# Spectral mixing weights in 4 KB rows: two half-partition loads per tile and block-diagonal stationaries

## The chip, the cores and the metric

One core of one Trainium2 chip runs the whole program. The metric is device time in microseconds of one launch; times are medians over runs. The kernel before takes 456.05 us (three runs: 455.77, 456.05, 456.72).

## What is computed

Linear attention with an exponential feature map, followed by a spectral mixing layer over the sequence. Cut to what matters:

```python
# q, k, v: (8 batches, 8 heads, 576, 64) f32; w_phi (64, 128)
phi(x) = concat(exp(p), exp(-p))          # p = x @ w_phi - max|x @ w_phi|
kv  = k_p^T v ; z = sum(k_p)              # per batch and head
x   = (q_p kv) / (q_p z)                  # (8, 576, 512): heads side by side
X   = rfft(x, axis=1)[:, :64]             # 64 modes
Yr  = Xr w_r - Xi w_i                     # per mode: (8 x 512) @ (512 x 512)
Yi  = Xr w_i + Xi w_r                     # w_r, w_i: (64, 512, 512) f32
u   = x + irfft(Y)
out = u + relu(u @ w_ch)                  # w_ch (512, 512)
```

The mode weights w_r and w_i are 64 x 512 x 512 floats each, 134 MB together; q, k and v are 9.4 MB each. Every weight is used once.

## The kernel before

The 512 input rows of each mode's matrix are the 8 heads times 64. The kernel treats them in four quarters g of 128 rows (two heads). The first quarter is split in its two heads, the others are whole.

**Attention loop** (lines 555 to 623). There are N = 32 units of work: 8 units of two batches and one head (quarter 0), then 24 units of one batch and two heads (quarters 1 to 3). Iteration n works on unit n (`feat_tok`, `feat_q`, `exps`, `ekq`), on unit n-1 (`kv_mm`, `num_mm`, `numer`) and on unit n-2 (`x_mm`). The order on each engine is the order in which this code is written (`manual_schedule`); the framework adds the waits. `vscale` (L270, L275), on POOL, scales v of unit n and writes `vaug`, which `kv_mm` of unit n (L286, TensorE) reads in iteration n+1. `numer` ends with the unit's part of x in `xs_all`. `x_mm` (L344) multiplies that by the cosine and sine columns `CF4` and ScalarE copies the result into `XT` (L369): the modes of x, with 32 columns per mode and part (real, imaginary; 8 batches), beside columns of zeros, so that a stationary of 32 columns fills either the upper or the lower half of a 32-row output block. There are two such buffers, `XT0` and `XT1`, used by quarters in turn. In iterations 28 to 33 `flip_early` and `times_w_early` do pieces of x @ w_ch; `inverse_matrix` runs in iterations 10 to 14.

**Weights** come in 32 groups (`weights`, L156): 8 groups of 16 modes for the two heads of quarter 0 (L167: four loads of 64 partitions), then 24 groups of 8 modes, `wr` and `wi` (L162: one load of 128 partitions each). The loads convert f32 to bf16 and are issued on POOL's queue. `wr` and `wi` have three buffers each (`NW = 3`): the load of group k+3 waits until `mode_mm` of group k (L390, TensorE, 16 matmuls at L416 per group) has read its buffer. `mode_sum` (VectorE) adds the result to `Yacc`. In the loop one group is multiplied per iteration once its quarter of x is there (`after`, L111: groups 0 to 3 from iteration 5, 4 to 7 from 9, 8 to 15 from 17, 16 to 21 from 25).

**POOL's order in one iteration** (from n = 4): the loads of q and k for a later pair of units (`load_qk`, L143, odd n), then the weight loads for which a buffer may become free (L585 to 587), then `vscale`. v is loaded from SP's queue (L127), and is not converted.

**The tail** (lines 785 to 819) multiplies the last ten groups, 22 to 31, and between them does the other x @ w_ch pieces (`flip_x`, `times_w`) and, for quarter 3, the turn of Y by batch (`by_batch`). After group 31 come the inverse transform and the output (lines 841 to 856).

Of the kernel before, what the change touches and what calls it, by code (L numbers as in the profile page):

```python
# [21 lines left out]
NCH = 5  # L22
# [4 lines left out]
def kernel(  # L27
# [11 lines left out]
    nc = tc.nc  # L39
# [14 lines left out]
    xs_all = pers.tile([128, B_ * NCH, DMODEL], BF16, name="xs_all")  # L54
# [8 lines left out]
    CF4 = const.tile([128, NCH, 4, 64], BF16, name="CF4")  # L63
# [3 lines left out]
    XTs = [XT0, XT1]  # L67
# [23 lines left out]
    def qk_pair(pool, i):  # L91
        return [pool.tile([128, 2, 10, D_], BF16, name=f"{nm}2_{i}") for nm in "qk"]
# [63 lines left out]
    def weights(k):  # L156
        g, gi = groups[k]
        wt = {}
        for ri, w in ((0, moe_w_r), (1, moe_w_i)):
            t = pw.tile([128, 8, DMODEL], BF16, name=f"w{'ri'[ri]}", tag=f"w{ri}")  # L160
            if gi >= 0:
                nc.gpsimd.dma_start(  # L162
                    t, w[8 * gi:8 * gi + 8, g * 128:(g + 1) * 128, :].rearrange("m p e -> p m e"))
            else:
                for x in range(2):
                    mx = 16 * (-1 - gi) + 8 * x
                    nc.gpsimd.dma_start(  # L167
                        t[64 * x:64 * x + 64],
                        w[mx:mx + 8, g * 64:(g + 1) * 64, :].rearrange("m p e -> p m e"))
            wt[ri] = t  # L170
        W[k] = wt
# [172 lines left out]
    def x_mm(st):  # L344
        psx = psum.tile([128, 2, 4, 64], F32, name="psx", tag="tx", bufs=1)
        XT = XTs[st["xt"]][:, 16:80, :].rearrange("p (x y b) m -> p x y b m", x=2, y=4)
        if "bs" in st:

            h = st["h"]
            for i, b in enumerate(st["bs"]):  # L350
                for c in range(NCH):
                    for x in range(2):
                        nc.tensor.matmul(
                            psx[64 * x:64 * x + 64, i, :, :],
                            lhsT=xs_all[:, b * NCH + c, h * 64:(h + 1) * 64],
                            rhs=CF4[:, c, :, :],
                            start=(c == 0), stop=(c == NCH - 1),
                        )
        else:
            g = st["g"]  # L360
            for c in range(NCH):
                nc.tensor.matmul(
                    psx[:, 0, :, :],
                    lhsT=xs_all[:, st["b"] * NCH + c, g * 128:(g + 1) * 128],
                    rhs=CF4[:, c, :, :],
                    start=(c == 0), stop=(c == NCH - 1),
                )
        for i, b in enumerate(st["bs"] if "bs" in st else (st["b"],)):
            nc.scalar.copy(  # L369
                XT[:, :, 0:2, b, :],  # L370
                psx[:, i, :, :].rearrange("d (x y) m -> d x y m", x=2),
            )
# [17 lines left out]
    def mode_mm(k, tag="yr"):  # L390
        g, gi = groups[k]
        XT = XTs[1 - g if k < 8 else g % 2]
        wt = W.pop(k)
        if gi < 0:
            psY = psum.tile([128, 2, DMODEL], F32, name="psY2", tag="pC", bufs=1)
            for par in range(2):
                for ri in range(2):
                    for j in range(4):
                        for x in range(2):
                            r = slice(64 * x, 64 * x + 64)  # L400
                            m = 16 * (-1 - gi) + 8 * x + 2 * j + par
                            c0 = (16, 0, 48, 32)[2 * ri + par]
                            nc.tensor.matmul(
                                psY[32 * j:32 * j + 32, x, :],
                                lhsT=XT[r, c0:c0 + 32, m],
                                rhs=wt[ri][r, 2 * j + par, :],
                                start=(par == 0 and ri == 0), stop=(par == 1 and ri == 1),
                            )
            return psY
        psY = psum.tile([128, DMODEL], F32, name="psY", tag=tag, bufs=1)  # L410
        for ri in range(2):
            for par in range(2):
                for j in range(4):
                    m = 8 * gi + 2 * j + par
                    c0 = (16, 0, 48, 32)[2 * ri + par]
                    nc.tensor.matmul(  # L416
                        psY[32 * j:32 * j + 32, :],
                        lhsT=XT[:, c0:c0 + 32, m],
                        rhs=wt[ri][:, 2 * j + par, :],
                        start=(par == 0 and ri == 0), stop=(par == 1 and ri == 1),  # L420
                    )
        return psY

# [26 lines left out]
    def zeros(i):  # L450
        for z in (0, 32, 64):
            nc.vector.memset(XTs[i][:, z:z + 16, :], 0.0)

    def setup():

# [73 lines left out]
    with tc.manual_schedule():  # L529
        load(S[0], "qk")  # L530
        setup()
        load(S[0], "v")
        load(S[1])
        zeros(1)
        casts(S[0], nc.vector)
        casts(S[1], nc.gpsimd, "q")
        load_qk(1)
        for t in AAs:
            nc.gpsimd.memset(t[:, 0, :, 1152:1216], 1.0)
        for t in e2s:  # L540
            nc.gpsimd.memset(t[64:128, :, NCH - 1:NCH], 1.0)
        casts(S[1], nc.gpsimd, "k")

        pa_first_cm.__exit__(None, None, None)
        pa_last_cm = tc.tile_pool(name="pa_last", bufs=1)
        pa_last = pa_last_cm.__enter__()
        qk2s[2] = qk_pair(pa_last, 2)
        for t in qk2s[2]:
            nc.gpsimd.memset(t[:, :, 9, :], 0.0)
        load_qk(2)  # L550
        weights(0)
        k_in = 1
        transp(S[0], "q")
        transp(S[0], "k")
        for n in range(N + 2):
            cur = S[n] if n < N else None
            prev = S[n - 1] if 0 <= n - 1 < N else None
            old = S[n - 2] if 0 <= n - 2 < N else None
            nxt = S[n + 1] if n + 1 < N else None
            if n + 2 < N:  # L560
                load(S[n + 2])
            if cur:
                feat_tok(cur, "k", "pB")
                feat_q(cur)
            if psY is not None:
                mode_sum(k_out, psY)
                psY = None
                k_out += 1
            if cur:
                rem_mm(cur)  # L570
                absmax(cur, "k")
                absmax(cur, "rem")
                exps(cur, "q")
            if nxt:
                transp(nxt, "q")
            if prev:
                kv_mm(prev)
                kv_cp(prev)
            if cur:
                ekq(cur, "k")  # L580
            if n < 4:
                vscale(cur)
            if n % 2 == 1 and 5 <= n < N - 5:
                load_qk((n + 5) // 2)
            while k_in < min(k_out + NW, 2 if n < 3 else 32):  # L585
                weights(k_in)
                k_in += 1
            if n in (1, 3):
                load_qk((n + 5) // 2)
            if n == 16:  # L590
                nc.gpsimd.dma_start(wchb, moe_w_ch.rearrange("(dc p) e -> p dc e", p=128))
            if cur and n >= 4:
                vscale(cur)
            if nxt:
                transp(nxt, "k")
            if cur:
                exps(cur, "k")
                exps(cur, "rem")
            if prev:
                num_mm(prev, 1)  # L600
                numer(prev, 0)
                num_mm(prev, 0)
                numer(prev, 1)
                numer(prev, 2)
            if old:
                x_mm(old)
            e = n - (N + 2 - N_EARLY)
            if e >= 0:
                sTe = flip_early(e)
            if cur:  # L610
                feat_tok(cur, "q", "pA")
                absmax(cur, "q")
                ekq(cur, "q")
            if n == 0:
                forward_matrix()
            if n == 2:
                zeros(0)
            if 10 <= n < 10 + NCH:
                inverse_matrix(n - 10)
            if e >= 0:  # L620
                times_w_early(e, sTe)
            if k_out < K_IN_ATTN and n >= after[k_out] + 2:
                psY = mode_mm(k_out)
# [161 lines left out]
    with tc.manual_schedule():  # L785
        plan = {22: 3, 23: 3, 24: 2, 25: 2, 26: 2, 27: 1, 28: 2, 29: 1, 30: 1, 31: 0}
        while k_out < 32:
            k = k_out
            gi = groups[k][1]
            while k_in < min(k_out + NW, 32):  # L790
                weights(k_in)
                k_in += 1
# [94 lines left out]
```

## Time and profile before

| | before |
|---|---|
| median of 3 runs | 456.05 us |
| span of the profiled execution | 456.7 us (its run is nearest to 456.72) |
| busy PE / VectorE / ScalarE / POOL | 301.7 / 292.0 / 261.8 / 198.8 us |
| mean rate of the DMA engines (as written) | 214 GB/s |
| read from HBM, written | 163.64 MB, 9.44 MB |
| POOL's loads (q0) | 75,728 packets, 76.75 MB |
| loop ends, `mode_mm(22)` starts | 331.07 us |
| last group, `mode_mm(31)` | 415.56 us |

The profile is of one execution. Its times count from the first instruction. "Busy" is the time in which an engine has an instruction at work; a share of busy time is an average over the loop, the tail and the output, which have different limits. The rate of the DMA engines counts bytes as written, so a converting load reads twice what is shown. For a load, "landing" is the moment at which its completion is signalled. In timelines the columns are start, duration, engine, line, operation, and in brackets the idle time before it and what ended that.

### The profile page before, as it was taken

To read this page: it belongs to the slowest core of one execution; us is meant where nothing else is said; L and a number is where in the kernel's file an instruction comes from. 1 tells how busy PE (TensorE), PEld (TensorE's weight loads), DVE (VectorE), ACT (ScalarE), POOL (GpSimd) and SP (SyncE) were. 2 spreads that over 40 slices of the span, in tenths; PEclk is the share of its full clock that TensorE was granted. 3 is DMA by queue.
4 is the path that set the end of the run, shared out by engine and by line. 5 is a ranking of instruction groups with operands and counts; after the bars stand their busy time and mean duration, and the time that the engine had idled before them with its cause. 6 is when DMAs were issued, how large, how long until landed. Compare 5 with 4: busy or idle time off the path is not lost.

```text
span 456.7 us, 11065 instructions
## 1 busy us (share of the span) xinstructions
PE 301.7 (66%) x4637; PEld 197.6 (43%) x4637; DVE 292.0 (64%) x418; ACT 261.8 (57%) x528; POOL 198.8 (44%) x251
## 2 busy tenths in 40 slices
PE   3476776833767677655555544755578878868993
PEld 2355565622555565544333432433344445433341
DVE  6578789844988779876666472776322273653873
ACT  4576887833686877865545452765334455644662
POOL 3956476445563256553435231443021212100993
PEclk9976899876886769998778595999999999998997
DMA  6999999999999999999999999999999999990697
GB/s 179 195 228 222 225 213 226 221 206 216 221 228 217 230 219 222 224 219 229 218 207 217 218 218 218 207 203 207 207 207 207 207 207 207 207 179 11 223 341 299
DMA packets 84417, 97.70 MB, mean 214 GB/s; under 512 B 3152, under 2 KB 77136, under 8 KB 84368
## 3 DMA queue, kind: packets, MB, share of 16 engines
q0 software_dynamic: 75728, 76.75, 101.1%
q1 hardware_dynamic: 8480, 20.19, 12.8%
q8 instruction: 36, 0.59, 0.5%
q14 instruction: 13, 0.11, 0.1%
q10 hardware_dynamic: 160, 0.07, 0.1%
HBM read 163.64 MB, written 9.44 MB: 379 GB/s over the span
## 4 chain that ended last, share of the span: by engine, by line
DMA 34%; issue 24%; DVE 17%; PE 11%; POOL 7%; ACT 3%; SPq 1%; DVEq 0%; POOLq 0%; ACTq 0%
DMA wi<-in_moe_w_i_dram 29%; DVE mkq L233 6%; DMA wr<-in_moe_w_r_dram 4%; DVE xs_all L336 2%; DVE nd L322 2%; DVE tB L315 2%; POOL vaug L270 2%; PE ptr L184 1%; PE psNB L305 1%; ACT AA L240 1%; PE kvz L286 1%; PE psB L753 1%; DVE of L776 1%; SPq L122 1%; POOL wr L162 1%
## 5 line engine op out<-in xcount | busy, mean ns | idle before, releaser
L270 POOL TENSOR_TENSOR vaug<-vn,ee 128x576 bf16<-128x576 f32 x64 | 72.7, 1155 | 63.3 <-ACT ee L255 50.2
L240 ACT ACTIVATE AA<-psT 128x1024 bf16<-128x1024 f32 x64 | 62.0, 1021 | 43.6 <-PE psT L208 43.1
L262 ACT ACTIVATE e<-mkq 64x4 f32<-64x4 f32 (+1 forms) x128 | 26.3, 206 | 61.5 <-DVE mkq L233 59.2
L244 ACT ACTIVATE AA<-psk 128x1024 bf16<-128x1024 f32 x64 | 61.4, 1010 | 0.0
L162 POOL DMA_DIRECT2D wr<-in_moe_w_r_dram x24 | 21.9, 912 | 86.6 <-PE psY L416 77.8
L416 PEld LDWEIGHTS <-XT 128*32 128x32 bf16 x384 | 17.1, 171 | 56.6 <-issue 46.4
L667 ACT CAST xw<-psW 128x1024 bf16<-128x1024 f32 x17 | 17.2, 1013 | 40.5 <-PE psW L665 34.6
L233 DVE TENSOR_REDUCE mkq<-psk 128x8 f32<-128x1024 f32 x32 | 38.8, 1213 | 0.7 <-PE psk L199 0.7
L233 DVE TENSOR_REDUCE mkq<-psq 128x8 f32<-128x1024 f32 x32 | 38.9, 1217 | 0.4 <-PE psq L199 0.4
L435 DVE TENSOR_TENSOR Yacc<-psY,Yacc 128x512 f32<-128x512 f32 x16 | 11.0, 689 | 42.5 <-PE psY L416 42.5
L416 PE MATMUL psY<-wi,XT 128*32 128x512 bf16 x192 | 18.0, 435 | 28.8 <-DMA wi<-in_moe_w_i_dram 28.8
L286 PE MATMUL kvz<-vaug,AA 64*128 64x65 bf16 x1152 | 29.2, 210 | 11.5 <-POOL vaug L275 9.8
L190 DVE COPY kT<-ptr 128x640 bf16<-128x640 bf16 x32 | 15.7, 492 | 32.5 <-PE ptr L184 32.5
L665 PE MATMUL psW<-wchb,sT 128*128 128x512 bf16 x136 | 33.5, 391 | 2.1 <-ACT xw L667 2.1
L315 DVE TENSOR_TENSOR tB<-psNB,e 128x650 f32<-128x650 f32 x32 | 26.7, 833 | 11.2 <-PE psNB L305 10.6
L305 PEld LDWEIGHTS <-AA 128*128 128x128 bf16 x640 | 29.0, 110 | 9.3 <-issue 8.9
L286 PEld LDWEIGHTS <-AA 64*128 64x128 bf16 x1152 | 25.1, 107 | 15.9 <-issue 11.8
L162 POOL DMA_DIRECT2D wi<-in_moe_w_i_dram x24 | 21.1, 880 | 23.8 <-PE psY L416 20.5
L322 DVE TENSOR_TENSOR nd<-psNA,tB 128x650 f32<-128x650 f32 x32 | 26.7, 835 | 4.1 <-DVE tB L315 0.5
L416 PE MATMUL psY<-wr,XT 128*32 128x512 bf16 x192 | 17.0, 424 | 18.0 <-DMA wr<-in_moe_w_r_dram 8.7
L336 DVE TENSOR_TENSOR xs_all<-nd,rden 128x640 bf16<-128x640 f32 x32 | 28.0, 874 | 1.1
L184 PE MATMUL ptr<-ident_b,k 128*128 128x128 bf16 x160 | 17.9, 257 | 14.8 <-DVE qT L190 12.6
(132 smaller groups left out, 705.4 us busy)
## 6 DMA issues: line engine op xcount, KB each, us to landing
wr<-in_moe_w_r_dram POOLq DMA_DIRECT2D x24, 1024.0 KB, 25.8
wi<-in_moe_w_i_dram POOLq DMA_DIRECT2D x24, 1024.0 KB, 29.4
wr<-in_moe_w_r_dram POOLq DMA_DIRECT2D x16, 512.0 KB, 15.9
wi<-in_moe_w_i_dram POOLq DMA_DIRECT2D x16, 512.0 KB, 19.6
out_dram<-of SPq DMA_DIRECT2D x16, 512.0 KB, 3.8
vn<-in_v_dram SPq DMA_DIRECT2D x24, 288.0 KB, 5.8
q<-in_q_dram POOLq DMA_DIRECT2D x12, 288.0 KB, 19.3
k<-in_k_dram POOLq DMA_DIRECT2D x12, 288.0 KB, 20.0
```

Of the source, the lines that this page charges most:

```text
L162: nc.gpsimd.dma_start(t, w[8 * gi:8 * gi + 8, g * 128:(g + 1) * 128, :].rearrange("m p e -> p m e"))
L233: nc.vector.tensor_reduce(out=o, in_=i, axis=AX.X, op=ALU.max, apply_absolute_value=True)
L240: nc.scalar.activation(AA[:, 0, ab, 0:1024].rearrange("f (x j p) -> f j x p", j=2, p=64), st["psT"].rearrange("f j (x p) -> f j x p", p=64 ...
L244: nc.scalar.activation(AA[:, 1, ab, 0:1024].rearrange("p (c j f) -> p j c f", c=4, j=2), st["psk"], ACT.Exp, scale=sc)
L270: nc.gpsimd.tensor_tensor(out=vaug[:, ab, :, 0:64], in0=st["v"], in1=ee[:, ab, :].unsqueeze(2).to_broadcast([128, 9, D_]), op=ALU.mult,)
L286: nc.tensor.matmul(kvz[:, hh, ab * 65:(ab + 1) * 65], lhsT=AA[r, 1, ab, 128 * j:128 * j + 128], rhs=vaug[r, ab, j, :], start=(j == 0), sto ...
L305: nc.tensor.matmul(p[:, hh, 65 * c:65 * c + 65], lhsT=AA[:, 0, ab, x:x + 128], rhs=kvzF[:, hh, ab * 65:(ab + 1) * 65], start=True, stop=True,)
L315: nc.vector.tensor_tensor(out=tB, in0=st["psNB"], in1=e2.unsqueeze(3).to_broadcast([128, 2, NCH, 65]), op=ALU.mult,)
L322: nc.vector.tensor_tensor(out=nd, in0=st["psNA"], in1=st["tB"], op=ALU.add)
L336: nc.vector.tensor_tensor(out=xo, in0=nd[:, :, :, 0:64], in1=rden.to_broadcast([128, 2, NCH, 64]), op=ALU.mult,)
L416: nc.tensor.matmul(psY[32 * j:32 * j + 32, :], lhsT=XT[:, c0:c0 + 32, m], rhs=wt[ri][:, 2 * j + par, :], start=(par == 0 and ri == 0), sto ...
L665: nc.tensor.matmul(ps[:, x, :], lhsT=sT[:, x, dc, :], rhs=wchb[:, dc, :], start=(dc == 0), stop=(dc == 3))
```

## The change

In the 24 groups of quarters 1 to 3 a weight tile is loaded by two DMAs instead of one. The first fills partitions 0 to 63 with the even modes of the group, the second 64 to 127 with the odd ones; partition p of a half takes rows 2p and 2p+1 of the quarter, which lie side by side in HBM, so that one row of the transfer is 4 KB of f32 (2 KB of bf16) instead of 2 KB (1 KB). Quarter 0 keeps its four loads of 2 KB rows per group.

The other operand has to match. `x_mm` for quarters 1 to 3 now makes, for rows of parity i and modes of parity y, a matmul with every second of 128 columns of x as stationary (64 columns) and every second column of `CF4` (4 x 32 columns) as moving operand: 2 x 5 x 2 = 20 matmuls of 128 columns per unit instead of 5 of 256. Two ScalarE copies of 64 partitions, one for each parity of the modes, take the place of one of 128. In `XT` the modes are now ordered by i, then by pair of modes, and the zeros stand block-diagonally: partitions 0 to 63 hold an even mode in the first 16 of 32 columns, partitions 64 to 127 an odd mode in the last 16. `mode_mm` keeps 16 matmuls of 32 columns per group; each now sums over 64 rows of two modes instead of 128 rows of one, and i takes the place of the mode's parity. `zeros_late` clears, on POOL, what quarter 0 left in the half blocks that have to be zero: `XT1` at the end of iteration 9, `XT0` at the end of iteration 13.

```diff
@@ weights
             if gi >= 0:
-                nc.gpsimd.dma_start(
-                    t, w[8 * gi:8 * gi + 8, g * 128:(g + 1) * 128, :].rearrange("m p e -> p m e"))
+                for y in range(2):
+                    nc.gpsimd.dma_start(
+                        t[64 * y:64 * y + 64].rearrange("p (m i) e -> p m (i e)", i=2),
+                        w[8 * gi + y:8 * gi + 8:2, g * 128:(g + 1) * 128, :].rearrange(
+                            "m (p i) e -> p m (i e)", i=2))
@@ x_mm
-            g = st["g"]
-            for c in range(NCH):
-                nc.tensor.matmul(
-                    psx[:, 0, :, :],
-                    lhsT=xs_all[:, st["b"] * NCH + c, g * 128:(g + 1) * 128],
-                    rhs=CF4[:, c, :, :],
-                    start=(c == 0), stop=(c == NCH - 1),
+            g, b = st["g"], st["b"]
+            for i in range(2):
+                for c in range(NCH):
+                    for y in range(2):
+                        nc.tensor.matmul(
+                            psx[64 * y:64 * y + 64, 0, :, 32 * i:32 * i + 32],
+                            lhsT=xs_all[:, b * NCH + c, g * 128 + i:(g + 1) * 128:2],
+                            rhs=CF4[:, c, :, y::2],
+                            start=(c == 0), stop=(c == NCH - 1),
+                        )
+            for y in range(2):
+                nc.scalar.copy(
+                    XT[64 * y:64 * y + 64, :, 2 * y:2 * y + 2, b, :],
+                    psx[64 * y:64 * y + 64, 0, :, :].rearrange("d (x y) m -> d x y m", x=2),
                 )
-        for i, b in enumerate(st["bs"] if "bs" in st else (st["b"],)):
+            return
+        for i, b in enumerate(st["bs"]):
@@ mode_mm
-            for par in range(2):
+            for i in range(2):
                 for j in range(4):
-                    m = 8 * gi + 2 * j + par
-                    c0 = (16, 0, 48, 32)[2 * ri + par]
                     nc.tensor.matmul(
                         psY[32 * j:32 * j + 32, :],
-                        lhsT=XT[:, c0:c0 + 32, m],
-                        rhs=wt[ri][:, 2 * j + par, :],
-                        start=(par == 0 and ri == 0), stop=(par == 1 and ri == 1),
+                        lhsT=XT[:, 16 + 32 * ri:48 + 32 * ri, 32 * i + 4 * gi + j],
+                        rhs=wt[ri][:, 2 * j + i, :],
+                        start=(i == 0 and ri == 0), stop=(i == 1 and ri == 1),
                     )
@@ new
+    def zeros_late(i):
+        for z in (16, 48):
+            nc.gpsimd.memset(XTs[i][64:128, z:z + 16, :], 0.0)
@@ attention loop, at the end of an iteration
+            if n in (9, 13):
+                zeros_late(1 if n == 9 else 0)
```

## The prediction, made before the result

> **What bounds the kernel now.** I read first the page's slices and DMA lines.
>
> ```profile
> DMA  6999999999999999999999999999999999990697
> GB/s 179 195 228 222 225 213 226 221 206 216 221 228 217 230 219 222 224 219 229 218 207 217 218 218 218 207 203 207 207 207 207 207 207 207 207 179 11 223 341 299
> ...
> wi<-in_moe_w_i_dram POOLq DMA_DIRECT2D x24, 1024.0 KB, 29.4
> ...
> wi<-in_moe_w_i_dram POOLq DMA_DIRECT2D x16, 512.0 KB, 19.6
> ```
>
> From the second slice until the weights end the DMA engines are full, and a load lands 20 to 29 us after its issue: a long queue. 207 GB/s is counted in written bf16, so twice that is read. This invites "make the rows cheaper". Two more views say what else hangs on this queue. First POOL's timeline at 100 us, where weights already come in half loads (the first quarter), then the first loads of the second quarter:
>
> ```profile
> 102.85 0.68 POOL L167 DMA_DIRECT2D wr<-in_moe_w_r_dram  x1 [1.33 <-DMA wi<-in_moe_w_i_dram]
> 104.71 0.68 POOL L167 DMA_DIRECT2D wi<-in_moe_w_i_dram  x1 [1.18 <-PE psx L362]
> 108.23 0.68 POOL L167 DMA_DIRECT2D wi<-in_moe_w_i_dram  x1 [2.84 <-DMA k<-in_k_dram]
> 108.92 2.27 POOL L270 TENSOR_TENSOR vaug<-vn,ee 128x576 bf16<-128x576 f32 x2
> ...
> 132.36 0.87 POOL L162 DMA_DIRECT2D wi<-in_moe_w_i_dram  x1 [0.21 <-PE rem L218]
> 135.26 1.15 POOL L270 TENSOR_TENSOR vaug<-vn,ee 128x576 bf16<-128x576 f32 x1 [2.02 <-ACT ee L255]
> ```
>
> An issue on POOL waits for a landing. The program's listing says which: POOL's loads take eight completion counters in turn, and each waits until the load eight before it has landed. The issue at 102.85 follows the landing at 102.57 of the load eight before, 108.23 follows 107.94. So at most eight loads are on their way, and what stands behind such an issue on POOL waits too: vscale (L270), and through vaug the kv matmuls (L286) of the next iteration. At 135.26 vscale waits for its own input only.
>
> Then TensorE around the end of the attention loop, and in the tail:
>
> ```profile
> 312.08 0.69 PE L416 MATMUL psY<-wi,XT 128*32 128x512 bf16 x8 [0.97 <-DMA wi<-in_moe_w_i_dram]
> ...
> 320.52 0.75 PE L286 MATMUL kvz<-vaug,AA 64*128 64x65 bf16 x36
> ...
> 331.07 0.69 PE L416 MATMUL psY<-wr,XT 128*32 128x512 bf16 x8 [0.67 <-ACT xw L388]
> ```
>
> ```profile
> 402.78 0.69 PE L416 MATMUL psY<-wr,XT 128*32 128x512 bf16 x8 [0.78 <-DVE sT L657]
> 404.63 0.69 PE L416 MATMUL psY<-wi,XT 128*32 128x512 bf16 x8 [1.16 <-DMA wi<-in_moe_w_i_dram]
> ```
>
> Until 312 mode_mm waits for weights. From 320.52 to 331.07 it is kv, numerators, x_mm, flip_early and their evacuations, one after another. From 331.07 to the end the order is set by compute: group 22 is used at 331.07 though its second half landed at 322.2, and only group 30 waits, 1.16 us. **So the tail can win 1.16 us from faster weights, no more; the rest of the time hangs on when kv_mm of the last unit starts (320.52).**
>
> **Part 1, rows of 4 KB.** In the trace's packet records starts on one engine lie 78.8 ns apart for a 2048-byte row read, 88.2 ns for the 2304-byte rows of q and k: 9.4 ns per 256 bytes and 3.6 ns per row. A 4096-byte row then takes 78.8 + 8 x 9.4 = 154 ns (taken). Ends: 150 ns (bytes alone) and 160 ns (the 4096-byte output rows stand 155 to 160 ns apart; two old rows are 157.6). A half load is 16 rows per engine plus 22 ns for its completion packet: 16 x 0.154 + 0.022 = 2.49 us, a group of four 9.95. Today a full load is 64 x 0.0788 + 0.022 = 5.065 us, and in the tail they do land 5.06 to 5.07 apart: 10.13 us a group. Gain **0.18 us a group**, 2.7 us by group 22.
>
> Half loads cost the queue nothing else: those of the first quarter land 2.50 to 2.55 us apart, half of 5.06. The Trainium skill (DMA: Bandwidth & Descriptors, Anatomy of one DMA) gives each DMA about 2 us of fixed cost; if 48 more loads paid it in the queue the estimate would be 96 us more. The trace disagrees with that here: the cost lies beside the next load's data.
>
> **Part 2, twice as many loads through eight counters.** POOL's issue time grows little: 0.88 to 0.93 us for 1024 rows, 0.68 to 0.72 for 512, so about 0.66 us for 256; 2.6 instead of 1.8 us a group. The counters cost more. Three groups were six loads; now they are twelve, and eight fit.
>
> *Iterations 11 to 13.* They issue q/k, group 8, group 9, q/k, group 10. Today group 10's second load goes out at 132.36. Now its fourth waits for the second half load of group 9, the same bytes as group 9's wr, which lands at 148.64 today, 148.4 with 1.5 x 0.18 off. Issue 0.3 to 0.5 after that, 0.66 us long: vscale of unit 13 starts at 149.5 instead of 135.26 and ends at 152.0. kv_mm(13), now at 141.32, starts there: +10.7. From kv_mm to the next head the rows take 6.4 to 7.2 us, so the loop runs about **10 us late** at iteration 14, and mode_mm(8) at 180.7 instead of 170.7. Until then no more weights may be asked for (three buffers). What is queued lands at 179.63 today (k of iteration 17), now about 179.1; the next half load is issued at 181.7 and flows some 1.3 us later. **The DMA queue, never empty before, is empty some 4 us**; less one v load (0.8 us) that falls into the gap, I take 3.5, bounds 0 and 6.
>
> *Afterwards* the loop has room (about 8 us compute against 10 to 12 us of DMA per iteration); late vscales are absorbed because eight loads, 13 to 20 us, are always queued. So group 22 lands at 322.19 + 3.5 - 2.7 = 323.0.
>
> *End of the loop.* Today iteration 31 issues group 24 at 313.08, when group 21 has been used, and vscale(31) follows at 315.95. Now group 24's fourth half load waits for group 22's fourth: 323.0 + 0.4 + 0.66 = 324.1, vscale ends at 326.6, kv_mm(31) starts at 326.7 instead of 320.52: **+6.2**.
>
> **Part 3, x_mm.** Per unit 20 matmuls of 128 columns replace 5 of 256 (0.71 us), and two copies of 64 partitions one of 128 (0.37 us each by the same 256 columns). Ends: 0.42 us (36 of L286 take 0.75) and 2.27 (20 of 256 columns, L353); by L199 (8 of 128 columns in 0.40) 1.0. In the loop psq is ready at 153.64 and first read at 155.15, which covers 1.5 us; flip_early's iterations (28 on) lose 0.4 us of a 1 us DMA wait. Uncovered is the last unit's, before mode_mm(22): +0.3 + 0.37 = 0.7; bounds 0 and 2. Against it the evacuation before it (ACT at 322.12, kv done at 321.27) no longer stands behind exponents: -0.5.
>
> **Part 4, the rest at nothing.** zeros_late: 2 KB per partition twice; a 512-byte POOL memset took 0.23 us, so some 2 us, where POOL then waits for counters (iteration 9) or for ee (13). mode_mm keeps 16 matmuls of the same shape and column stride. Without cover these cost 2 us once.
>
> **Sum** against the profiled execution (456.7 us): +6.2 +0.7 -0.5 = +6.4 at mode_mm(22), 337.5. The tail keeps its compute; group 25 is asked for at 338.4 while group 24 lands at 342.44 + 3.5 - 3.1 = 342.8, so the queue stays filled, by 4 us. The 1.16 us wait goes. 456.7 + 6.4 - 1.2 = 461.9. The median shown, 456.05, lies 0.6 below this execution: **461.3 us** (all times below are put on the median).
>
> **Rivals.**
> - *The rows win, the counters never bite* (faster). 456.7 - 2.5 (group 21) + 0.7 - 1.2 = 453.7, so 453.1. It decides if loads land before POOL comes to the counter. For it: today's loop from 180 us mostly waits for psY buffers (77.8 us), not for loads. Against: the waits at 102.85 and 108.23, with the same four loads a group. 0.08.
> - *No gap near 180*: group 22 lands at 319.5, vscale(31) still waits for it; kv_mm(31) +2.7, end 458.3, so 457.7. For it: v fills the gap, or iterations 14 to 17 recover. 0.15.
> - *Half loads gain nothing or rows cost more*. At 2.54 us, as the first quarter's halves: group 22 at 325.9, +2.9 on the forecast, 464.2; at 160 ns a row 2.58 us, about 466.4. For it: no load of today writes 2 KB rows into 64 partitions, and the halves reach 206 GB/s where 154 ns needs 213. The Trainium skill (SBUF — State Buffer, Door 1: The DMA port swizzle) lets 64 partitions reach half of the ports, which by its 436 GB/s would be 218, just enough; no row here shows the cap. 0.22.
>
> **Chances.** Forecast 0.52, the three rivals 0.08, 0.15, 0.22, dearer x_mm with strided operands (two to five us more) 0.03. Range 457.0 to 467.0: it leaves out the faster case, half of a tenth beside it, and 0.06 above. A measurement of this kernel can tell about 0.2% from no change. Faster by more 0.08, within 0.08 (the low end of the no-gap case), slower 0.84.
>
> **What would show it.** Half loads of the later quarters 2.49 us apart; POOL's vscale(13) behind weight issues near 149 us, the head of iteration 17 10 us late; a short hole in the DMA line near 180 us; vscale(31) right behind the last issue of group 24, some 10 us after mode_mm(21); no wait for wi at group 30. I am wrong if vscale(13) stays near 135 us, if rows stand 158 ns apart or more, or if the tail waits for weights.

## The result, and the profile after

The changed kernel takes **469.88 us** (median of six runs, 465.9 to 471.85) against 456.16 us of the kernel before, measured beside it: ratio **1.0278, 95% interval 1.0242 to 1.0314**. Slower was right; the forecast of 461.3 and its upper bound of 467 were too low. The profiled execution has a span of 468.9 us (its time is 470.93), 12.2 more than the span of before. In every run listed with both, the time is about 2 us above the span. The execution of before that was profiled, span 456.7, therefore took some 458.6 us and not the 456.72 or so that was taken ahead of the result, some 2.5 us above its median. The two spans can be compared directly: the prediction's sum of 461.9 stands against 468.9, **7.0 us short** (by the medians 8.6). Some kernels below have executions more than 1.5% above their fastest: the medians count them, the ratios leave them out.

The page of after, slices and DMA lines; the first line is the clock of before, for comparison:

```profile
PEclk9976899876886769998778595999999999998997
...
PEclk9995899787886867998958576888759999998997
DMA  6999999999999996999999999999999999970697
GB/s 183 187 228 218 221 204 228 219 214 221 206 233 210 233 199 120 220 234 211 231 210 233 210 225 228 214 211 211 211 194 166 193 211 210 212 142 1 210 339 291
...
wr<-in_moe_w_r_dram POOLq DMA_DIRECT2D x64, 512.0 KB, 18.0
```

The rows do what they should: 211 GB/s where 207 stood, and in the packet records 4 KB rows start 154 ns apart. But one slice, near 180 us, shows 120 GB/s, and there are three weaker ones between 340 and 375. These three lie in the tail, where no matmul waits for a load; they cost nothing that the trace shows. The stretches in and behind the first dip (columns: stretch, length, busy time and count of each engine, granted clock, share and rate of the DMA engines):

```profile
177.60:183.20 5.60, 4.96 (x79) 3.47 (x77) 5.25 (x8) 3.86 (x11) 3.96 (x6) 0.73 0.23 61
183.20:190.00 6.80, 4.81 (x123) 3.89 (x124) 5.73 (x9) 5.49 (x12) 5.27 (x8) 1.00 1.08 190
```

For 5.6 us the engines carry 61 GB/s. POOL's timeline says why (start, duration, operation, idle time before it and what ended that):

```profile
142.84 0.61 POOL L163 DMA_DIRECT2D wr<-in_moe_w_r_dram  x1 [2.18 <-DMA wi<-in_moe_w_i_dram]
146.17 0.61 POOL L163 DMA_DIRECT2D wi<-in_moe_w_i_dram  x1 [2.72 <-DMA wr<-in_moe_w_r_dram]
148.46 0.61 POOL L163 DMA_DIRECT2D wi<-in_moe_w_i_dram  x1 [1.68 <-DMA wr<-in_moe_w_r_dram]
149.09 2.27 POOL L273 TENSOR_TENSOR vaug<-vn,ee 128x576 bf16<-128x576 f32 x2
...
181.70 1.29 POOL L163 DMA_DIRECT2D wr<-in_moe_w_r_dram  x2 [1.58 <-PE psY L425]
```

Each of the first three issues waits 1.7 to 2.7 us for the landing of a load; the load eight before the issue at 148.46 landed at 148.18. vscale(13), behind them, starts at 149.09 (its exponents were there at 136.44), `mode_mm(8)` at 180.70, and only then is group 11 asked for. The same at the end of the loop:

```profile
325.95 0.61 POOL L163 DMA_DIRECT2D wi<-in_moe_w_i_dram  x1 [0.38 <-DMA wi<-in_moe_w_i_dram]
326.58 2.27 POOL L273 TENSOR_TENSOR vaug<-vn,ee 128x576 bf16<-128x576 f32 x2
```

And TensorE from there into the tail. The first line is group 23 in before, which had kv_mm(31) at 320.52 and group 22 at 331.07; the others are after:

```profile
340.72 0.69 PE L416 MATMUL psY<-wr,XT 128*32 128x512 bf16 x8
...
329.10 0.76 PE L289 MATMUL kvz<-vaug,AA 64*128 64x65 bf16 x36 [1.97 <-POOL vaug L278]
...
341.05 1.09 PE L425 MATMUL psY<-wr,XT 128*32 128x512 bf16 x8 [0.67 <-ACT xw L399]
...
346.93 3.19 PE L680 MATMUL psW<-wchb,sT 128*128 128x512 bf16 x7 [0.22 <-issue]
...
351.34 1.89 PE L680 MATMUL psW<-wchb,sT 128*128 128x512 bf16 x8 [0.37 <-ACT xw L682]
...
354.02 0.69 PE L425 MATMUL psY<-wr,XT 128*32 128x512 bf16 x8
```

The step from group 22 to group 23 has grown from 9.65 to 12.97 us, and no wait explains it: the instructions themselves last longer, 3.19 us for seven matmuls at L680 where eight take 1.89 just after. The windows, on the grid on which the granted clock changes (3.413 us), show the clock:

```profile
310.28:313.70 3.42, 1.51 (x41) 1.38 (x41) 3.08 (x5) 3.31 (x9) 0.61 (x1) 1.00 1.13 214
313.70:317.11 3.41, 3.03 (x23) 1.37 (x27) 1.77 (x3) 0.85 (x5) 1.79 (x3) 0.50 1.12 211
...
327.35:330.76 3.41, 1.15 (x49) 1.11 (x49) 0.00 (x0) 1.12 (x3) 1.69 (x3) 1.00 1.12 211
330.76:334.18 3.42, 2.38 (x37) 1.88 (x33) 2.87 (x5) 0.73 (x2) 0.00 (x0) 0.50 1.13 214
337.59:341.00 3.41, 1.43 (x10) 0.74 (x9) 0.42 (x1) 1.32 (x3) 0.00 (x0) 1.00 1.12 211
341.00:344.42 3.42, 2.52 (x22) 1.39 (x22) 0.69 (x1) 0.00 (x0) 1.97 (x4) 0.50 0.91 163
```

The first number after the length is TensorE's busy time, the third from the end its clock. After each window shown with TensorE busy 1.15 to 1.51 of 3.41 us the clock is 0.50; after the last of these it stays there up to 351.24. In before it is 1.00 from 285 to 411 us (the run of nines in its line of slices). One more line is group 30 in the tail, where before waited 1.16 us for `wi`; its first matmuls wait for VectorE, and the `wi` ones follow without a wait:

```profile
416.04 0.67 PE L425 MATMUL psY<-wr,XT 128*32 128x512 bf16 x8 [0.78 <-DVE sT L672]
```

### The profile page after: what moved, and what is told of

It is laid out like the page before. It is cut to its first block, busy times and chain, and to the rows that moved or that the text cites. A ratio compares the mean times of both kernels' runs of the same rounds, so it can differ in the third digit from the quotient of the medians.

```text
span 468.9 us, 11866 instructions
## 1 busy us (share of the span) xinstructions
PE 316.0 (67%) x4979; PEld 212.0 (45%) x4997; DVE 293.3 (63%) x418; ACT 270.8 (58%) x552; POOL 217.7 (46%) x303
## 4 chain that ended last, share of the span: by engine, by line
PE 28%; DMA 24%; DVE 19%; ACT 11%; POOL 7%; issue 7%; SPq 1%; DVEq 0%; ACTq 0%; POOLq 0%
DMA wr<-in_moe_w_r_dram 15%; DMA wi<-in_moe_w_i_dram 8%; PE psW L680 6%; DVE mkq L236 4%; PE psY L425 3%; POOL vaug L273 3%; DVE xs_all L339 3%; ACT AA L243 3%; DVE nd L325 3%; ACT AA L247 2%; DVE tB L318 2%; PE pt L669 2%; PE psZY L720 2%; PE kvz L289 2%; DVE zy L733 2%
## 5 line engine op out<-in xcount | busy, mean ns | idle before, releaser
L163 POOL DMA_DIRECT2D wr<-in_moe_w_r_dram x48 | 30.1, 630 | 93.7 <-PE psY L425 61.7
L163 POOL DMA_DIRECT2D wi<-in_moe_w_i_dram x48 | 29.6, 624 | 51.0 <-DMA wi<-in_moe_w_i_dram 17.0
L289 PEld LDWEIGHTS <-AA 64*128 64x128 bf16 x1152 | 26.5, 107 | 48.1 <-issue 43.9
L680 PE MATMUL psW<-wchb,sT 128*128 128x512 bf16 x127 | 34.4, 406 | 2.3 <-ACT xw L682 1.7
L308 PEld LDWEIGHTS <-AA 128*128 128x128 bf16 x640 | 30.8, 114 | 7.3 <-issue 6.8
L298 ACT CAST kvzF<-kvz 128x260 bf16<-128x260 f32 x32 | 12.1, 379 | 37.3 <-PE kvz L289 37.3
L425 PEld LDWEIGHTS <-XT 128*32 128x32 bf16 x384 | 16.6, 166 | 26.6 <-issue 16.3
L211 PE MATMUL psT<-qT,w 64*128 64x512 bf16 x64 | 14.6, 444 | 20.0 <-DVE mkq L236 19.8
L672 DVE COPY sT<-pt 128x1024 bf16<-128x1024 bf16 x17 | 11.7, 691 | 23.8 <-PE pt L669 23.7
```

The source lines that it names most:

```text
L163: nc.gpsimd.dma_start(t[64 * y:64 * y + 64].rearrange("p (m i) e -> p m (i e)", i=2), w[8 * gi + y:8 * gi + 8:2, g * 128:(g + 1) * 128, :] ...
L289: nc.tensor.matmul(kvz[:, hh, ab * 65:(ab + 1) * 65], lhsT=AA[r, 1, ab, 128 * j:128 * j + 128], rhs=vaug[r, ab, j, :], start=(j == 0), sto ...
L308: nc.tensor.matmul(p[:, hh, 65 * c:65 * c + 65], lhsT=AA[:, 0, ab, x:x + 128], rhs=kvzF[:, hh, ab * 65:(ab + 1) * 65], start=True, stop=True,)
L425: nc.tensor.matmul(psY[32 * j:32 * j + 32, :], lhsT=XT[:, 16 + 32 * ri:48 + 32 * ri, 32 * i + 4 * gi + j], rhs=wt[ri][:, 2 * j + i, :], st ...
L680: nc.tensor.matmul(ps[:, x, :], lhsT=sT[:, x, dc, :], rhs=wchb[:, dc, :], start=(dc == 0), stop=(dc == 3))
```

## The experiments

The theory after the result: the number of loads, through the eight counters and POOL's order, makes vscale late at two places (iterations 11 to 13 and 31), and TensorE's clock falls in the thin stretch that follows the second. Rivals: 4 KB rows or half loads are dear in themselves; x_mm is dear; the clock falls for a reason of its own. Ratios are to the kernel before, measured beside each run.

**1. Half loads without the rows.** The kernel before, with each load of L162 cut in two:

```diff
-                nc.gpsimd.dma_start(
-                    t, w[8*gi:8*gi+8, g*128:(g+1)*128, :].rearrange("m p e -> p m e"))
+                for y in range(2):
+                    nc.gpsimd.dma_start(t[64*y:64*y+64],
+                        w[8*gi:8*gi+8, g*128+64*y:g*128+64*y+64, :].rearrange("m p e -> p m e"))
```

> The kernel before with each weight load of quarters 1 to 3 cut into two of 64 partitions, rows still 2 KB, nothing else changed. Counter theory (eight loads on their way, vscale behind the issues): the same hole near 180 us (5 to 6 us) and the same late vscale(31), halves landing 2.54 us apart, plus some 3 to 5 us of slow TensorE clock around 330 to 350 us: 467 to 472 us. Rival (the loss of the change comes from x_mm, from the 4 KB rows or from the block-diagonal stationaries): 456 to 457 us, as before.

Measured: 467.89 us, ratio 1.0233 (1.0182 to 1.0285). vscale(13) in its POOL timeline, and the wait rows of kv_mm in before and in this run (total us, number of waits, the longest):

```profile
147.68 0.68 POOL L163 DMA_DIRECT2D wi<-in_moe_w_i_dram  x1 [1.64 <-DMA wr<-in_moe_w_r_dram]
148.38 2.27 POOL L273 TENSOR_TENSOR vaug<-vn,ee 128x576 bf16<-128x576 f32 x2
```

```profile
PE kvz L286 <- POOL vaug L275: 9.8, 2, 6.1
...
PE kvz L289 <- POOL vaug L278: 46.8, 16, 9.3
```

The same bytes in the same rows, twice as many loads: 10.6 us. Its half loads land 2.54 us apart, half of the 5.06 of a full load in before, so filling only 64 partitions costs the queue no time. The number of loads gives most of the loss. (The waits add up to more than the loss. Some 19 us of them lie between 200 and 300 us, and as much stays there in run 10, where most of the loss is gone.)

**2. The rows without the half loads.** The kernel after with one load of 128 partitions per tile:

```diff
-                for y in range(2):
-                    nc.gpsimd.dma_start(...)
+                h = 8 * gi + 4 * (g % 2)
+                nc.gpsimd.dma_start(
+                    t.rearrange("p (m i) e -> p m (i e)", i=2),
+                    w[h:h+4, g//2*256:g//2*256+256, :].rearrange("m (p i) e -> p m (i e)", i=2))
```

> The changed kernel with one load of 128 partitions per tile in 4 KB rows: four modes and 256 rows instead of eight modes and 128 rows, so that the bytes and the row length are those of the change, but the rows read are not the ones that the products need; the output is not the reference's. x_mm, stationaries and zeros_late are those of the change. Counter theory: no hole, vscale(13) near 135 us, loads landing 4.95 us apart, 452 to 454.5 us, faster than before by 0.4 to 0.9%. Rival (the rows or x_mm cost the time): 460 us or more.

Measured: 457.39 us, ratio 0.9991 (0.9953 to 1.0029); the profiled execution has a span of 452.9. vscale(13) waits for its exponents again, not for a counter:

```profile
134.52 2.27 POOL L273 TENSOR_TENSOR vaug<-vn,ee 128x576 bf16<-128x576 f32 x2 [1.82 <-ACT ee L258]
```

The loss is gone; the rival (dear rows, dear x_mm) is out as the main cause. The gain that I expected (452 to 454.5) is not there; run 7 shows why.

**3 and 4. vscale ahead of POOL's loads in every iteration**, in after and, as a control, in before:

```diff
-            if n < 4:
+            if n < 4 or cur:
                 vscale(cur)
```

> The changed kernel with vscale written ahead of the loads of its iteration in all iterations. Counter theory: a vscale then stands only behind the issues of the iteration before; vscale(13) at 135 to 140 us, vscale(14) still behind group 10's fourth half near 149 us, at most 1 us of hole, kv_mm of the last unit as early as before, 453 to 457 us. Rival (the hole comes from the loads themselves, whatever stands behind them): 464 us or more.

> The kernel before with vscale ahead of the loads, the control for the run beside it. Counter theory: iterations 9 and 10, where vscale stands behind the first quarter's half loads today, run 5 to 8 us earlier, but the DMA queue is full all the time, so the end moves by no more than 0.4% either way: 454 to 458 us. Rival (vscale's place bounds the kernel before too): faster by 5 us or more.

Measured: 469.97 (1.0242, 1.0177 to 1.0308) and 462.25 (1.0103, 1.0072 to 1.0133). Both expectations missed. POOL's timeline keeps the written order: with vscale ahead, loads that are free to go stand behind vscale, which waits for exponents. Its timeline in after with the move:

```profile
176.40 2.27 POOL L273 TENSOR_TENSOR vaug<-vn,ee 128x576 bf16<-128x576 f32 x2 [4.97 <-ACT ee L258]
...
184.59 2.26 POOL L273 TENSOR_TENSOR vaug<-vn,ee 128x576 bf16<-128x576 f32 x2 [4.39 <-ACT ee L259]
...
186.93 1.29 POOL L163 DMA_DIRECT2D wr<-in_moe_w_r_dram  x2
```

Group 11 is issued at 186.93, though `mode_mm(8)` started at 179.44; in after it went out 1.0 us behind the start of `mode_mm(8)`. So these two runs do not speak against the counters; the move trades one wait for the other and could not separate them.

**5 and 6. The same move at one place each**: in iteration 31 only, and in iterations 8 to 13 only (`n == 31`, `8 <= n <= 13` in the condition).

> The changed kernel with vscale ahead of the loads in iteration 31 alone. The prediction's end-of-loop term, undone: the hole near 180 us stays, kv_mm of the last unit starts 3 to 4 us earlier (near 325.5 us), and if TensorE's clock then stays up around 340 to 350 us the tail's first step takes 9.7 us instead of 13: 462 to 466 us. Rival (the end of the loop hangs on the landing of group 22 and not on vscale): 469 to 471 us, as changed.

> The changed kernel with vscale ahead of the loads in iterations 8 to 13 alone. The prediction's first term, undone: mode_mm of group 8 some 7 us earlier (near 173 us), the hole near 180 us gone or under 1 us, group 22 landing 4 to 6 us earlier, the late vscale(31) unchanged: 463 to 467 us. Rival (the hole is absorbed later, the loss is at the end alone): 469 to 471 us.

Measured: 465.99 (1.0205, 1.0142 to 1.0268) and 463.26 (1.0148, 1.0108 to 1.0187), both within what was expected. With iteration 31 changed, kv_mm(31) starts 9.0 us behind the iteration's head (325.21 behind 316.17) instead of 11.0; with 8 to 13 changed, `mode_mm(8)` starts at 174.06 instead of 180.70. By the traces both places are real. The first has the larger gain, 1.30% against 0.73%, but the intervals of the two runs overlap, and 0.73% alone is at the edge of the noise. From kv_mm(31) to group 23 both still take some 23.5 us, where before took 20.2.

**7. x_mm without the new loads.** The kernel after with the loads of before.

> The changed kernel with the loads of the kernel before (one of 128 partitions, 2 KB rows): only x_mm with its 20 matmuls and two copies, the stationaries and zeros_late are new. The weights then lie in another order than the stationaries expect, so the output is not the reference's. Counter theory: 456.2 + 0.5 to 1.5 us, within 0.4% of before. Rival (x_mm and its strided operands are what costs): 462 us or more.

Measured: 460.13, ratio 1.0058 (1.0034 to 1.0081): 2.6 us, above what I expected. In the trace x_mm itself is as forecast: 20 matmuls take 0.78 us at full clock (run 11) where five took 0.71, and here from kv_mm(31) to group 22 it is 10.75 us instead of 10.55. From run 7 to run 2 only the loads' rows differ: 0.67% less, 3.1 us, which is their gain (group 22 lands at 318.15 instead of 322.08). Run 2 is level with before because the two cancel.

**8 and 9. vscale of units 8 to 13 and 28 to 31 on VectorE**, in after and, as control, in before. In these units nothing that TensorE reads stands behind POOL's loads, and no load stands behind vscale:

```diff
+        eng = nc.vector if 8 <= n <= 13 or n >= 28 else nc.gpsimd
-            nc.gpsimd.tensor_tensor(out=vaug[:, ab, :, 0:64], ...)
+            eng.tensor_tensor(out=vaug[:, ab, :, 0:64], ...)
-        nc.gpsimd.tensor_copy(vaug[:, :, :, 64], ee)
+        eng.tensor_copy(vaug[:, :, :, 64], ee)
```

> Kernel after, with vscale of units 8 to 13 and 28 to 31 on VectorE instead of POOL (same operation; its place in the written order is kept). POOL's loads go on waiting for the counters, but nothing that TensorE reads stands behind them in these units. Theory (counters hold vscale on POOL): vscale(13) starts within 2 us of its exponents instead of 12.6 later, mode_mm(8) before 175 instead of 180.7, no hole in the DMA line near 180, kv_mm(31) by 323 instead of 329.1. VectorE gets 2 to 2.5 us more per unit in iterations where it is busy 7 of 8.5 us, which the control run shows by itself. Against that control: 3 us faster to 2 us slower; 454 to 461 in all. Rival (the loss is in the loads, the rows or x_mm themselves): 7 us or more slower than the control, 464 or more.

> Control: kernel before with the same move, vscale of units 8 to 13 and 28 to 31 on VectorE. Here the counters do not hold vscale, so the move brings nothing and costs VectorE 2 to 2.5 us in ten iterations, of which some is covered: 456 to 461 (+0 to +1.1%).

Measured: 469.07 (1.0226, 1.0150 to 1.0302) and 463.60 (1.0144, 1.0086 to 1.0203). Both are slower than expected. By the ratios after is 0.8% (3.7 us) above its control, with overlapping intervals: more than the theory's 2 us, less than the rival's 7. The time alone decides nothing; the traces say where it goes. Up to the last iterations the theory holds: `mode_mm(8)` starts at 174.09, the hole near 180 is gone, and group 22 lands at 319.24, against 325.66 in after and 320.87 in the control. The stretch that held the hole, in after with vscale on VectorE:

```profile
177.60:183.20 5.60, 4.20 (x113) 3.48 (x108) 4.90 (x9) 4.53 (x11) 4.47 (x7) 1.00 1.10 189
```

Then two things hide it. Iterations 28 to 30 take 12 us each in both kernels instead of 10.2: VectorE is part of their chain, and the control's kv_mm(31) starts at 327.69, 7.2 later than in before, so the move is bad there. And behind kv_mm(31) (326.84 with after, 327.69 in the control) after is at half clock again: 12.84 us from group 22 to 23 against 9.51. The difference between the two lies wholly behind kv_mm(31), where both have the same program but for x_mm, L425 and the loads; kv_mm(31) waits for vscale in neither.

**10. Both single moves of 5 and 6 together.**

> Kernel after with vscale ahead of POOL's loads in iterations 8 to 13 and in iteration 31, the two single moves together. If the two places are separate losses, the gains add: 469.9 - 6.6 - 3.9 = 459.4, range 458 to 461. Rival (both moves remove the same lateness, the second is worth nothing once the first is made): 462.5 to 464.

Measured: 461.15, ratio 1.0065 (1.0025 to 1.0105), which is 459.7 by the ratio. The single gains, 1.30% and 0.73%, add to 2.03%; together they give 2.13%. Two separate losses, about 9.7 us.

The profile also shows what the theory did not expect. kv_mm(31) starts at 321.16 without a wait for vscale, and the clock falls behind it all the same (windows of 3.413 us, then kv_mm(31), group 22, a group of L680 and group 23):

```profile
328.39:331.80 3.41, 1.59 (x12) 0.82 (x15) 0.42 (x1) 1.15 (x3) 0.00 (x0) 1.00 1.11 208
331.80:335.22 3.42, 2.58 (x24) 1.65 (x20) 0.69 (x1) 0.00 (x0) 2.26 (x4) 0.50 1.13 212
```

```profile
321.16 0.90 PE L289 MATMUL kvz<-vaug,AA 64*128 64x65 bf16 x36
...
331.63 1.02 PE L425 MATMUL psY<-wr,XT 128*32 128x512 bf16 x8 [0.67 <-ACT xw L399]
...
337.01 3.62 PE L680 MATMUL psW<-wchb,sT 128*128 128x512 bf16 x8
...
344.61 0.69 PE L425 MATMUL psY<-wr,XT 128*32 128x512 bf16 x8
```

From group 22 to 23 it is 12.98 us, as in after.

**11. The clock.** The kernel after with matmuls added that fill TensorE's gaps in iterations 32 and 33:

```diff
+    def fill(m):
+        ps = psum.tile([128, DMODEL], F32, name="psF", tag="yr", bufs=1)
+        for _ in range(m):
+            nc.tensor.matmul(ps, lhsT=wchb[:, 0, 0:128], rhs=wchb[:, 0, :], start=True, stop=True)
...
+            if n == N: fill(8)      # ahead of kv_mm(31)
+            if n >= N: fill(3)      # behind x_mm, and again behind flip_early
+            if n == N + 1: fill(3)  # behind times_w_early
```

> Kernel after with matmuls added whose result nobody reads, in iterations 32 and 33 where TensorE waits (8 of 512 columns ahead of kv_mm(31), 3 in each of five waits for evacuations after it). In the trace of after the granted clock halves in the 3.4 us windows that follow a window with TensorE busy under 1.55 us (1.51, 1.47, 1.15, 1.43 us), and 10 us at half clock, from 341.0 on, cost the first step of the tail 3.3 us. Theory (the clock follows the busy share of the window before): with the gaps filled the clock is 1.0 from kv_mm(31) to group 23, the step from group 22 to 23 takes 9.7 to 10.3 instead of 13.0, kv_mm(31) to mode_mm(22) 10.5 to 12 instead of 11.95; in all 465 to 467.5 against 469.9. Rival (the clock falls for another reason, after the late loop): the step stays near 13 and the time is 469.5 to 472.

Measured: 465.68, ratio 1.0187 (1.0131 to 1.0242). More work, 4.2 us less time by the medians; the intervals of the two ratios just touch. Its windows in the stretches shown above, and the two groups:

```profile
327.35:330.76 3.41, 3.04 (x45) 1.51 (x44) 0.00 (x0) 1.34 (x5) 1.13 (x2) 0.85 1.12 211
330.76:334.18 3.42, 3.19 (x50) 1.98 (x49) 2.52 (x4) 0.83 (x3) 0.00 (x0) 1.00 1.13 213
...
337.59:341.00 3.41, 3.35 (x29) 1.38 (x26) 0.42 (x1) 0.59 (x1) 0.02 (x1) 1.00 1.12 211
341.00:344.42 3.42, 1.73 (x23) 1.33 (x20) 1.77 (x3) 0.00 (x0) 2.47 (x4) 1.00 1.03 183
```

```profile
339.98 0.69 PE L430 MATMUL psY<-wr,XT 128*32 128x512 bf16 x8
...
349.66 0.69 PE L430 MATMUL psY<-wr,XT 128*32 128x512 bf16 x8
```

kv_mm(31) starts at 329.63, as late as in after; from there to group 22 it is 10.35 us instead of 11.95, and to group 23 another 9.68 instead of 12.97. The rival (the clock falls after a late loop whatever TensorE does) is out: the loop is as late, and the clock stays.

**12. All three mended**: vscale of units 8 to 13 on VectorE, ahead of the loads in iteration 31, and the filling matmuls.

> Kernel after with three edits: vscale of units 8 to 13 on VectorE (where the control showed no lateness up to iteration 28), vscale ahead of POOL's loads in iteration 31, and the filling matmuls of iterations 32 and 33. Theory (the whole loss is POOL's waits for counters at these two places and the half clock after them): group 22 lands by 320 and mode_mm(8) by 175, as with vscale of ten units on VectorE; iterations 28 to 31 take 10.4 each again, so kv_mm(31) starts at 319 to 321 as in before, the step from group 22 to 23 takes 9.7; in all 454 to 458, about the time of before (ratio 0.995 to 1.004). Rival (half loads or x_mm cost something else that stays): 460 or more.

Measured: 459.92, ratio 1.0059 (1.0037 to 1.0081), above the theory's 454 to 458 and at the rival's edge. The parts do what they should: `mode_mm(8)` at 175.18, group 22 lands at 320.51, 10.04 us from group 22 to 23. But kv_mm(31) starts at 325.04, not at 319 to 321. vscale(31) had ended at 319.52; what stands ahead of kv_mm(31) now is my filler and a window at half clock (320.52 to 323.94):

```profile
321.44 1.49 PE L398 MATMUL psWe<-wchb,sTe 128*128 128x512 bf16 x3 [0.38 <-issue]
322.72 2.39 PE L405 MATMUL psF<-wchb 128*128 128x512 bf16 x8
325.04 0.75 PE L290 MATMUL kvz<-vaug,AA 64*128 64x65 bf16 x36
```

In run 11 these eight matmuls ran while kv_mm(31) had to wait anyway; here that wait is gone and they cost 2.3 us. What else stays is within the noise of these runs. No version of the change beat the kernel before.

## Why the prediction was wrong

| step | forecast | measured in after |
|---|---|---|
| 4 KB row, half load | 154 ns, 2.49 us | 154 ns, 2.49 us |
| vscale(13), kv_mm(13) | 149.5, 152.0 | 149.09, 151.60 |
| `mode_mm(8)` | 180.7 | 180.70 |
| hole in the DMA queue | 3.5 (0 to 6) | 5.6 us at 61 GB/s |
| group 22 landed | 323.0 | 325.66 |
| vscale(31), kv_mm(31) | 324.1, 326.7 | 326.58, 329.10 |
| `mode_mm(22)` | 337.5 | 341.05 |
| `mode_mm(22)` to `mode_mm(31)` | 84.49 - 1.16 = 83.3 | 86.34 |
| wait at group 30 | gone | gone |

*Rows: right.* Their gain by group 22 was, if anything, more than the 2.7 us: group 10 lands 1.6 us sooner than before, and from group 11 to 22 another 2.6 are won.

*Counters and both late places: right*, to half a microsecond up to 180 us. Runs 1, 5, 6 and 10 bear the mechanism out. zeros_late is as small as taken: its two memsets take 1.83 us, and one vscale waited 0.17 us for them.

*The hole: mis-sized.* The last load ahead of it landed at 178.43 (forecast 179.1), the first half load of group 11 at 187.13, 5.43 after its issue; I had 1.3 + 2.49 = 3.8 for that. The rate in slices of 0.5 us from 172 to 192 shows where it goes:

```profile
GB/s 80 67 159 373 173 184 210 134 143 184 187 65 0 0 0 0 0 37 203 304 46 0 119 193 160 86 176 217 209 209 213 225 205 213 201 205 217 209 218 269
```

Nothing moves from 178 to 180.5, then a v load, and group 11 from 183 on: the start took about what I had, 1.3 us. The first rows then came at 86 to 193 GB/s for 2.5 us; why is not shown. The lead over before turns from 1.6 us at group 10 into a lag of 6.1 at group 11, 7.7 instead of 3.3. Of that, the greater gain of the rows gives back part: **+2.7 us** at group 22 and, since vscale(31) waits for it, about +2.4 at kv_mm(31).

*The tail keeps its compute: this step failed.* I took the rows of before from kv_mm(31) on as they were, and they had been measured at full clock. In after TensorE waits 2 us for vscale(31) and then again and again for evacuations; two windows (1.15 and 1.43 us busy) are too thin, and what follows each runs at half clock: **+1.2 us** to `mode_mm(22)` (11.95 where I had 10.75) and **+3.3 us** from group 22 to 23. Run 11 shows that the thin windows do it: with them filled the two steps take 10.35 and 9.68. With 0.3 less in the rest of the tail and 0.4 more after group 31 the sum is 2.4 + 1.2 + 3.3 - 0.3 + 0.4 = 7.0, the whole shortfall. I did not read the granted clock of the stretch whose durations I carried over; the range had no term for it.

What makes these windows thin is only in part shown. From kv_mm(31) to group 23 it is 20.0 to 20.4 us in before and in runs 2, 7 and 9, some 21.5 in runs 1 and 4, and 23.4 to 26.1 in all six profiles that have both the half loads and the new x_mm and no filler (after and runs 3, 5, 6, 8 and 10). The wait for vscale(31) does not decide it: kv_mm(31) starts without one in runs 3, 5, 8 and 10, and waits 2.75 us in run 1. The stretch is thin in every kernel. In before its thinnest window (322.37 to 325.78) has TensorE busy for 1.70 us, and the clock stays; in run 10 it is 1.59, and the clock falls. Why half loads and the new x_mm lose it only together stays open.

*x_mm: its own size right, its whole not.* +0.2 us on the end of the loop, but run 7 costs 2.6. Its profile has half clock at 310 to 314 and 317 to 324, where before has 1.00, and its mean clock is 0.855 against 0.883. That x_mm leaves TensorE's windows emptier would fit: behind it TensorE waits 0.83 us for the evacuation where before waits 0.46. But this execution, at 457.88 us, is the fastest of its ten, and no run here takes x_mm's share of the clock apart; that stays open.

By the ratios: new x_mm +2.6, rows -3.1, twice as many loads +13.1 (run 2 to after, 2.87%). Of this the two late vscales are some 9.7 (run 10) and the clock in the tail some 4 (run 11). Run 10 keeps the slow step, so the two add up, to 13.1 within the noise.

## What to carry to other kernels

Before cutting loads in two, count how many are on their way and what stands behind their issue on the same engine: bytes and rows were right here, and the number of loads decided. An engine's order cuts both ways: moving the late instruction ahead of the loads in every iteration made the loads late instead; at the two chosen places it paid. And durations carried over from another trace hold only at its granted clock. Look at the clock, and at how thinly TensorE is busy in the windows just ahead: a stretch that is thin in before may lose its full clock when the program around it changes.

## What was not expected of the hardware

The granted clock changes on a fixed grid of 3.413 us. Up to 430 us it falls from 1.0 to 0.5 eighteen times in the trace of after and fifteen times in that of before, each time after a window with TensorE busy for 2.01 us or less of 3.41. From 22 us on no window under 1.6 us of busy time at full clock was followed by another at full clock; between 1.6 and 2.01 us some were (in before the one from 315.54 to 318.96, with 1.62) and some were not. The Trainium skill (TensorE: Matmul & The Clock Gate, Part 1: The HAM clock gate) has the clock fall after at least one idle window of about 3.4 us. The length agrees; but the windows here need not be idle, and under 1.6 of 3.41 us of busy time was always too little in these two traces. Filling such windows with matmuls that nobody reads was worth 4.2 us by the medians (run 11).

A load that found the queue empty took 5.43 us to land (issue at 181.70, landing at 187.13), where in the full queue half loads land 2.49 us apart. About 1.3 us of it, from the issue to the first bytes at 183, is a start that the full queue hides.
